# A decode step whose last weight load is cut along the partitions: six transfers over 96, 2, 4, 6, 8 and 12 partitions, the columns before it in pieces of 12 and 3

## Chip, core and metric

The kernel runs on one core of a Trainium2 chip. The metric is the device time of one execution in microseconds; before the change it is 232.49 us (median of 3 runs, 232.40 to 232.57).

## What is computed

One decode step for B = 2 tokens of width 512. The layer norm of x feeds an attention over the last 4096 cached positions (32 query heads, 8 key/value heads, head size 128) and a gated ReLU feed-forward of width 1792; both results are added to x. All data are float32. Cut to what matters:

```python
xn = _layernorm(x)
q = (xn @ wq).reshape(2, 1, 32, 128)
p = softmax(q . k_cache[last 4096] * 128 ** -0.5)
o = p . v_cache[last 4096]
h = relu(xn @ W_gate) * (xn @ W_up)
return x + o.reshape(2, 1, 4096) @ wo + h @ W_down
```

The weight wo has 4096 rows of 512 numbers, 8 MB in all.

## The kernel before

Nearly all of the 95 MB that the kernel reads (wq, the feed-forward weights, the cached keys and values, wo) are loaded by SP's DMA queue, in the order in which they are used, into a ring of four buffers (`RING = 4`, tag "ring"). A load into a buffer is issued once the work on the buffer's previous content is done. The order on TensorE is the order of the code (a manual schedule): q, gate and up, then for four groups of heads the transposes of the keys (L255), the scores (L268), the softmax and the weighted sum of the values (L332), and at the end the projections.

The end of the program is what the change touches. The tile y_ps sums everything that goes to the output: x itself (L412), 14 blocks of W_down (wd) and 32 blocks of wo. `project` (L417 to L422) adds one block with four matmuls. Each float32 matmul has two records in the trace, so a block has eight of MATMUL and eight of LDWEIGHTS: 112 each for wd, 256 each for wo. Before the last projections stand the values of the last group (`values`, L332), `gather` (L348), `finish` (L357) and `spread_heads` (L362), which makes the left-hand side oT.

wo comes in two halves, wo0 and wo1, one ring buffer each: 4 MB, 128 partitions by NJ = 16 columns of 512 numbers (a column is one block of `project`, 256 KB). wo0 comes in one transfer. wo1 comes in five, cut along the columns at 8, 12, 14 and 15 (L431 to L434):

```python
for r, cuts in ((0, (0, NJ)), (1, (0, 8, 12, 14, 15, NJ))):
    wt = ring.tile([P, NJ, D], F32, name=f"wo{r}", tag="ring")
    for j0, j1 in zip(cuts, cuts[1:]):
        nc.sync.dma_start(wt[:, j0:j1], wo_rows(r, j0, j1))
    for j in range(NJ):
        project(oT[:, r, j], wt[:, j], (r, j) == (R - 1, NJ - 1))
```

A matmul on a column waits for the transfer that brings that column, whole. After the last column VectorE copies y_ps to yo (L438) and SP stores it (L439). The transfers' completions are counted on eight semaphores that are used in turn.

Of the kernel before, what the change touches and what calls it, by code (L numbers as in the profile page):

```python
# [20 lines left out]
def kernel(  # L21
# [12 lines left out]
    nc = tc.nc  # L34
    P = 128
# [12 lines left out]
    R = HKV // C  # L48
# [20 lines left out]
    def load(name, src, shape):  # L69
        t = ring.tile(shape, F32, name=name, tag="ring")  # L70
        nc.sync.dma_start(t, src)
        return t
# [12 lines left out]
    def load_kv(cache, name, g, a):  # L85
        r, b = divmod(g, B)
        base = cache[b, r * C + 2 * a, SK - W:SK, :]
        run = J * DH
        src = bass.AP(
            tensor=cache.tensor, offset=base.offset, ap=[[run, PK], [SK * DH, 2], [1, run]]  # L90
        )
        return load(f"{name}{g}_{a}", src, [P, run])


    NJ = HQ * DH // (R * P)
# [3 lines left out]
    def wo_rows(r, j0, j1):  # L99
        rows = NJ * P  # L100
        return wo[r * rows:(r + 1) * rows, :].rearrange("(p j) e -> p j e", p=P)[:, j0:j1, :]
# [84 lines left out]
    for kc in range(KC):  # L186
        for r in range(R):
            for c in range(C):
                n = r * C + c
# [169 lines left out]
    def spread_heads(r):  # L359
        op = ps_1.tile([P, NJ, B], F32, name=f"op{r}", tag="misc")  # L360
        for e in range(NE):
            nc.tensor.matmul(  # L362
                op, spread[:, e].rearrange("h k e -> h (k e)"),
                osb[r][:, :, e * NJ:(e + 1) * NJ].rearrange("h b j -> h j b"),
                start=(e == 0), stop=(e == NE - 1),
            )
        nc.vector.tensor_copy(oT[:, r, :, :, 0], op)
# [19 lines left out]
    for a in range(NP):  # L387
        kwork(0, a, load_kv(k_cache, "k", 0, a))
    for g in range(1, NG):
        for a in range(NP):  # L390
            kt_in = load_kv(k_cache, "k", g, a)
            v_in = load_kv(v_cache, "v", g - 1, a)
            kwork(g, a, kt_in, [softmax(g - 1)] if a == 0 else [])
            if a:
                gather(g - 1, a - 1)
            elif g % B == 1 and g > 1:
                spread_heads((g - 2) // B)
            values(g - 1, a, v_in)
        gather(g - 1, NP - 1)
        finish(g - 1)  # L400
# [16 lines left out]
    def project(lhsT, w, stop):  # L417
        for e in range(Q):
            nc.tensor.matmul(  # L419
                y_ps[32 * e:32 * e + 17, :], lhsT.rearrange("p b s -> p (b s)")[:, 0:17],  # L420
                w[:, e * P:(e + 1) * P], start=False, stop=stop,
            )  # L422
# [5 lines left out]
    for k in range(FB):  # L428
        project(hT[:, k], dw[:, k], False)
    spread_heads(R - 1)  # L430
    for r, cuts in ((0, (0, NJ)), (1, (0, 8, 12, 14, 15, NJ))):  # L431
        wt = ring.tile([P, NJ, D], F32, name=f"wo{r}", tag="ring")
        for j0, j1 in zip(cuts, cuts[1:]):
            nc.sync.dma_start(wt[:, j0:j1], wo_rows(r, j0, j1))  # L434
        for j in range(NJ):
            project(oT[:, r, j], wt[:, j], (r, j) == (R - 1, NJ - 1))
    yo = work.tile([P, P], F32, name="yo", tag="yo", bufs=1)
# [30 lines left out]
```

## Time and profile before

| | |
|---|---|
| median of 3 runs | 232.49 us |
| the profiled execution's own time | 232.63 us |
| its span, first to last instruction | 230.8 us |
| TensorE busy | 180.2 us (78%) |
| VectorE, ScalarE busy | 66.3 us (29%), 48.3 us (21%) |
| data moved | 95.21 MB, 413 GB/s over the span |
| mean granted TensorE clock | 0.936 of full speed |

The span leaves out 1.8 us of the execution's time around the instructions. "PE" is TensorE's matmuls and "PEld" its weight loads, which run beside them; "SPq" is SP's sequencer, which issues the transfers. [...] "DMA share" is the mean busy share of the core's 16 DMA engines. The end of a matmul is modelled, so each record is about 0.27 us long although the next one starts earlier.

### The profile page before, as it was taken

To read this page: it belongs to the slowest core of one execution; us is meant where nothing else is said; L and a number is where in the kernel's file an instruction comes from. 1 tells how busy PE (TensorE), PEld (TensorE's weight loads), DVE (VectorE), ACT (ScalarE), POOL (GpSimd) and SP (SyncE) were. 2 spreads that over 40 slices of the span, in tenths; PEclk is the share of its full clock that TensorE was granted. 3 is DMA by queue.
4 is the path that set the end of the run, shared out by engine and by line. 5 is a ranking of instruction groups with operands and counts; after the bars stand their busy time and mean duration, and the time that the engine had idled before them with its cause. 6 is when DMAs were issued, how large, how long until landed. Compare 5 with 4: busy or idle time off the path is not lost.

```text
span 230.8 us, 4036 instructions
## 1 busy us (share of the span) xinstructions
PE 180.2 (78%) x1828; PEld 109.7 (48%) x1828; DVE 66.3 (29%) x131; ACT 48.3 (21%) x81; POOL 5.4 (2%) x21
## 2 busy tenths in 40 slices
PE   0066961749999889998899699889979964888393
PEld 0031230249666573664483566458456522247281
DVE  0320021014444561441472233158034133010000
ACT  2000100004444551440351243044033102100000
POOL 8000000000000000000000000000000000000000
PEclk9999797697999999999999799999999998899678
DMA  7999999999999999999999999999999999999980
GB/s 273 426 403 443 437 432 411 454 435 415 420 452 426 420 423 450 420 429 420 435 432 430 426 432 426 429 437 426 429 426 440 420 437 435 417 435 420 406 341 35
DMA packets 3964, 95.21 MB, mean 413 GB/s; under 512 B 452, under 2 KB 460, under 8 KB 876
## 3 DMA queue, kind: packets, MB, share of 16 engines
q1 hardware_dynamic: 3900, 94.90, 96.4%
q8 instruction: 14, 0.23, 0.4%
q10 hardware_dynamic: 48, 0.07, 0.1%
q14 instruction: 2, 0.02, 0.0%
HBM read 94.96 MB, written 0.00 MB: 412 GB/s over the span
## 4 chain that ended last, share of the span: by engine, by line
DMA 52%; PE 40%; DVE 4%; issue 1%; SPq 1%; ACT 1%
DMA k<-in_A_k_cache_dram 37%; PE pk L255 21%; DMA wo<-in_A_wo_dram 11%; PE s L268 8%; PE o L332 5%; DMA x<-in_A_x_dram 4%; PE q_ps L190 3%; PE pp L312 1%; PE oa L348 1%; SPq L434 1%; DVE kT L244 1%; DVE pt L313 1%; ACT p L301 1%; DVE on L244 0%; DVE m L277 0%
## 5 line engine op out<-in xcount | busy, mean ns | idle before, releaser
L255 PE MATMUL pk<-ident,k 128*128 128x128 f32 x512 | 68.0, 287 | 6.4 <-DMA k<-in_A_k_cache_dram 6.3
L255 PEld LDWEIGHTS pk<-ident,k 128*128 128x128 f32 x512 | 58.2, 146 | 21.2 <-issue 17.1
L244 DVE COPY kT<-pk 128x512 f32<-128x512 f32 x64 | 44.2, 691 | 52.6 <-PE pk L255 46.7
L244 ACT COPY kT<-pk 128x512 f32<-128x512 f32 x64 | 37.5, 586 | 81.5 <-PE pk L255 81.5
L332 PE MATMUL o<-v,pt 128*32 128x512 f32 x256 | 31.0, 615 | 0.0
L268 PE MATMUL s<-kT,qz 128*32 128x512 f32 x256 | 30.9, 598 | 0.0
L332 PEld LDWEIGHTS o<-v,pt 128*32 128x32 f32 x256 | 11.0, 113 | 14.6 <-issue 9.9
L190 PE MATMUL q_ps<-wq,xnT 128*32 128x512 f32 x64 | 11.9, 914 | 2.8 <-DMA wq<-in_A_wq_dram 2.3
L419 PE MATMUL y_ps<-wo,oT 128*17 128x128 f32 x256 | 10.1, 323 | 5.0 <-DMA wo<-in_A_wo_dram 4.8
L268 PEld LDWEIGHTS s<-kT,qz 128*32 128x32 f32 x256 | 7.0, 109 | 11.9 <-issue 11.5
L348 PE MATMUL oa<-on,pick 128*16 128x128 f32 x64 | 8.3, 273 | 4.1 <-DVE on L244 3.3
L419 PEld LDWEIGHTS y_ps<-wo,oT 128*17 128x17 f32 x256 | 7.9, 116 | 7.0 <-DMA wo<-in_A_wo_dram 6.0
L244 DVE COPY on<-o 128x512 f32<-128x512 f32 x4 | 2.8, 692 | 29.0 <-PE o L332 29.0
L348 PEld LDWEIGHTS oa<-on,pick 128*16 128x16 f32 x64 | 5.8, 97 | 11.1 <-DVE on L244 7.0
L177 PE MATMUL xt_ps<-ident,xn 32*128 32x32 f32 x4 | 1.0, 299 | 12.9 <-DVE xn L172 12.9
L217 PE MATMUL u_ps<-wu,xnT 128*32 128x448 f32 x32 | 4.6, 735 | 6.3 <-DMA wu<-in_B_W_up_dram 6.3
L190 PEld LDWEIGHTS q_ps<-wq,xnT 128*32 128x32 f32 x64 | 2.7, 154 | 11.3 <-issue 7.1
L244 ACT COPY on<-o 128x512 f32<-128x512 f32 x4 | 2.3, 586 | 25.5 <-PE o L332 25.5
L301 ACT ACTIVATE p<-s,nm 128x1024 f32<-128x1024 f32 x4 | 4.5, 1115 | 12.5 <-DVE nm L296 12.5
L177 PEld LDWEIGHTS xt_ps<-ident,xn 32*128 32x128 f32 x4 | 0.8, 206 | 12.8 <-issue 12.8
L312 PE MATMUL pp<-ident,p 128*128 128x128 f32 x32 | 4.9, 279 | 2.4 <-ACT p L301 1.5
L313 DVE TENSOR_TENSOR pt<-pp,own 128x512 f32<-128x512 f32 x8 | 5.4, 690 | 3.4 <-PE pp L312 3.4
(71 smaller groups left out, 61.5 us busy)
## 6 DMA issues: line engine op xcount, KB each, us to landing
k<-in_A_k_cache_dram SPq DMA_DIRECT2D x8, 4096.0 KB, 29.2
v<-in_A_v_cache_dram SPq DMA_DIRECT2D x8, 4096.0 KB, 31.2
wq<-in_A_wq_dram SPq DMA_DIRECT2D x2, 4096.0 KB, 17.5
wo<-in_A_wo_dram SPq DMA_DIRECT2D x1, 4096.0 KB, 31.5
wg<-in_B_W_gate_dram SPq DMA_DIRECT2D x1, 3584.0 KB, 30.2
wu<-in_B_W_up_dram SPq DMA_DIRECT2D x1, 3584.0 KB
wd<-in_B_W_down_dram SPq DMA_DIRECT2D x1, 3584.0 KB, 27.9
wo<-in_A_wo_dram SPq DMA_DIRECT2D x1, 2048.0 KB, 21.6
```

What stands on the lines that cost most here:

```text
L190: nc.tensor.matmul(q_ps[r][32 * c:32 * c + 32, :], xnT[:, 0, kc, :], wqt[kc // 2][:, kc % 2, n * 512:(n + 1) * 512], start=(kc == 0), stop ...
L217: nc.tensor.matmul(dst[32 * c:32 * c + 32, :], xnT[:, 1, kc, :], wt[:, kc, c * FQ:(c + 1) * FQ], start=(kc == 0), stop=(kc == KC - 1),)
L244: (nc.vector.tensor_copy if turn[0] % 2 else nc.scalar.copy)(dst, src)
L255: nc.tensor.transpose(pk[:, u * P:(u + 1) * P], kt_in[:, j * P:(j + 1) * P], ident)
L268: nc.tensor.matmul(ss[g][32 * q:32 * q + 32, :], qz[:, g, 32 * n:32 * n + 32], kt[:, h, q * 512:(q + 1) * 512], start=(a == 0 and s1 == 0 ...
L301: nc.scalar.activation(p, both, AF.Exp, bias=nm, scale=SCALE, accum_out=l)
L312: nc.tensor.transpose(pp[:, u], pv[:, lo:lo + P], ident)
L313: nc.vector.tensor_tensor(pts[g][:, jh].rearrange("p n u k -> p u n k"), pp.rearrange("p u (n k) -> p u n k", k=HK), own.rearrange("p h i ...
L332: nc.tensor.matmul(o[32 * q:32 * q + 32, :], pts[g][:, jh, n].rearrange("p u k -> p (u k)"), v[:, lo:lo + 512], start=(s1 == 0 and jh == 0 ...
L348: nc.tensor.matmul(oa[g], pick[:, u, 8 - 8 * a:24 - 8 * a], ons[a][:, u], start=(a == 0 and u == 0), stop=(a == NP - 1 and u == 3),)
L419: nc.tensor.matmul(y_ps[32 * e:32 * e + 17, :], lhsT.rearrange("p b s -> p (b s)")[:, 0:17], w[:, e * P:(e + 1) * P], start=False, stop=stop,)
L434: nc.sync.dma_start(wt[:, j0:j1], wo_rows(r, j0, j1))
```

## The change

The last column of wo1 (column 15, 256 KB) is cut along the partitions into six transfers, of 96, 2, 4, 6, 8 and 12 partitions; each brings 2 KB a partition. Columns 0 to 14 now come in two pieces, of 12 and of 3 columns, where there were four (8, 4, 2 and 1). The number of bytes, the buffers and the matmuls stay as they were.

```diff
+    LAST = (96, 2, 4, 6, 8, 12)
+    assert sum(LAST) == P
...
-    for r, cuts in ((0, (0, NJ)), (1, (0, 8, 12, 14, 15, NJ))):
+    for r, cuts in ((0, (0, NJ)), (1, (0, 12, 15, NJ))):
         wt = ring.tile([P, NJ, D], F32, name=f"wo{r}", tag="ring")
         for j0, j1 in zip(cuts, cuts[1:]):
-            nc.sync.dma_start(wt[:, j0:j1], wo_rows(r, j0, j1))
+            src = wo_rows(r, j0, j1)
+            p0 = 0
+            for n in (P,) if (r, j1) != (R - 1, NJ) else LAST:
+                nc.sync.dma_start(wt[p0:p0 + n, j0:j1], src[p0:p0 + n])
+                p0 += n
         for j in range(NJ):
             project(oT[:, r, j], wt[:, j], (r, j) == (R - 1, NJ - 1))
```

On SP, at the program's end (wo_1674 is wo0, wo_1740 is wo1; DMAHW0 to DMAHW7 are the eight semaphores of the transfers; a shape is partitions x numbers a partition):

```order
 L71 DMA wd<-in_B_W_down_dram 128x7168 [waits DMAHW1_49,PE_49]
-L434 DMA wo_1674<-in_A_wo_dram 128x8192 [waits DMAHW2_49,PE_49]
-L434 DMA wo_1740<-in_A_wo_dram 128x4096 [waits DMAHW3_49,PE_49]
-L434 DMA wo_1740<-in_A_wo_dram 128x2048
-L434 DMA wo_1740<-in_A_wo_dram 128x1024
-L434 DMA wo_1740<-in_A_wo_dram 128x512 x2
-L439 DMA out_dram<-yo 4x2x128 [waits DMAHW4_49,DVE_49]
```

```order
+L441 DMA wo_1674<-in_A_wo_dram 128x8192 [waits DMAHW2_49,PE_49]
+L441 DMA wo_1740<-in_A_wo_dram 128x6144 [waits DMAHW3_49,PE_49]
+L441 DMA wo_1740<-in_A_wo_dram 128x1536
+L441 DMA wo_1740<-in_A_wo_dram 96x512
+L441 DMA wo_1740<-in_A_wo_dram 2x512
+L441 DMA wo_1740<-in_A_wo_dram 4x512
+L441 DMA wo_1740<-in_A_wo_dram 6x512 [waits DMAHW4_49]
+L441 DMA wo_1740<-in_A_wo_dram 8x512 [waits DMAHW5_49]
+L441 DMA wo_1740<-in_A_wo_dram 12x512 [waits DMAHW6_49]
+L447 DMA out_dram<-yo 4x2x128 [waits DMAHW7_49,DVE_49]
```

The five transfers of wo1 have become eight, and three of them wait for the semaphore that they take over: the one over 6 partitions for the last load of values (DMAHW4), the one over 8 partitions for wd (DMAHW5), the one over 12 partitions for wo0 (DMAHW6).

On TensorE, the projections of wo before the change:

```order
L419 MATMUL y_ps<-wo_1674,oT 17x128 [waits DMAHW6_49]
L419 MATMUL y_ps<-wo_1674,oT 17x128 x63
L419 MATMUL y_ps<-wo_1740,oT 17x128 [waits DMAHW7_49,DVE_49]
L419 MATMUL y_ps<-wo_1740,oT 17x128 x31
L419 MATMUL y_ps<-wo_1740,oT 17x128 [waits DMAHW0_49]
L419 MATMUL y_ps<-wo_1740,oT 17x128 x15
L419 MATMUL y_ps<-wo_1740,oT 17x128 [waits DMAHW1_49]
L419 MATMUL y_ps<-wo_1740,oT 17x128 x7
L419 MATMUL y_ps<-wo_1740,oT 17x128 [waits DMAHW2_49]
L419 MATMUL y_ps<-wo_1740,oT 17x128 x3
L419 MATMUL y_ps<-wo_1740,oT 17x128 [waits DMAHW3_49]
L419 MATMUL y_ps<-wo_1740,oT 17x128 x3
```

and with it:

```order
L423 MATMUL y_ps<-wo_1674,oT 17x128 [waits DMAHW6_49]
L423 MATMUL y_ps<-wo_1674,oT 17x128 x63
L423 MATMUL y_ps<-wo_1740,oT 17x128 [waits DMAHW7_49,DVE_49]
L423 MATMUL y_ps<-wo_1740,oT 17x128 x47
L423 MATMUL y_ps<-wo_1740,oT 17x128 [waits DMAHW0_49]
L423 MATMUL y_ps<-wo_1740,oT 17x128 x11
L423 MATMUL y_ps<-wo_1740,oT 17x128 [waits DMAHW4_49,DMAHW5_49,DMAHW3_49,DMAHW6_49,DMAHW2_49,DMAHW1_49]
L423 MATMUL y_ps<-wo_1740,oT 17x128 x3
```

The matmuls are the same and stand in the same order. The waits ahead of columns 8, 12 and 14 are gone, the first wait now stands for 12 columns, and the wait ahead of column 15 is for six semaphores.

## Rows read from the trace of the kernel before

**Rows 1.** The page, 40 slices of the span: granted clock and DMA share, in tenths.

```profile
PEclk9999797697999999999999799999999998899678
DMA  7999999999999999999999999999999999999980
```

**Rows 2.** Chain of waits from 200 us: start us, us, what.

```profile
200.41 0.33 SPq L434
...
200.79 0.43 SPq L434
...
201.73 0.43 SPq L434
...
202.21 24.94 DMA wo<-in_A_wo_dram
...
227.19 0.46 PE y_ps L419 x8
```

**Rows 3.** DMA issues of wo1, in order: KB each, us from issue to landing.

```profile
wo<-in_A_wo_dram SPq DMA_DIRECT2D x1, 2048.0 KB, 21.6
wo<-in_A_wo_dram SPq DMA_DIRECT2D x1, 1024.0 KB, 23.8
wo<-in_A_wo_dram SPq DMA_DIRECT2D x1, 512.0 KB, 24.6
wo<-in_A_wo_dram SPq DMA_DIRECT2D x2, 256.0 KB, 24.9
```

**Rows 4.** Timeline of PE and SP at the end: start us, us [idle before <-releaser].

```profile
207.38 3.25 PE L419 MATMUL y_ps<-wd,hT 128*17 128x128 f32 x112
...
217.11 9.85 PE L419 MATMUL y_ps<-wo,oT 128*17 128x128 f32 x248 [4.58 <-DMA wo<-in_A_wo_dram]
...
227.19 0.41 PE L419 MATMUL y_ps<-wo,oT 128*17 128x128 f32 x8 [0.23 <-DMA wo<-in_A_wo_dram]
...
227.99 0.69 SPq L439 DMA_DIRECT2D out_dram<-yo  x1
```

**Rows 5.** Stretches: us, busy by engine (count), granted clock, DMA share, GB/s.

```profile
207.50:210.50 3.00, 3.00 (x112) 2.85 (x106) 0.34 (x1) 0.00 (x0) 0.00 (x0) 1.00 0.96 415
...
215.10:218.50 3.40, 1.39 (x28) 1.13 (x32) 0.00 (x0) 0.00 (x0) 0.00 (x0) 0.50 1.01 431
218.50:221.90 3.40, 3.40 (x72) 2.71 (x68) 0.00 (x0) 0.00 (x0) 0.00 (x0) 0.50 0.96 396
```

**Rows 6.** Stretches of the last microseconds, same columns.

```profile
222.00:223.00 1.00, 1.00 (x46) 0.99 (x40) 0.00 (x0) 0.00 (x0) 0.00 (x0) 1.00 0.99 379
223.00:224.00 1.00, 1.00 (x46) 0.99 (x40) 0.00 (x0) 0.00 (x0) 0.00 (x0) 1.00 0.73 287
224.00:225.00 1.00, 1.00 (x44) 0.96 (x40) 0.00 (x0) 0.00 (x0) 0.00 (x0) 1.00 0.47 184
225.00:226.00 1.00, 0.85 (x33) 0.57 (x28) 0.00 (x0) 0.00 (x0) 0.00 (x0) 1.00 0.38 135
```

**Rows 7.** Timeline of PE, two earlier waits for keys.

```profile
129.46 1.89 PE L255 MATMUL pk<-ident,k 128*128 128x128 f32 x9 [2.08 <-DMA k<-in_A_k_cache_dram]
...
169.55 1.50 PE L255 MATMUL pk<-ident,k 128*128 128x128 f32 x12 [1.25 <-DMA k<-in_A_k_cache_dram]
```

**Rows 8.** Stretches behind these two waits, columns as in rows 5.

```profile
130.00:133.00 3.00, 3.00 (x16) 3.00 (x15) 1.38 (x2) 0.70 (x2) 0.00 (x0) 0.50 0.94 404
133.00:134.00 1.00, 1.00 (x11) 1.00 (x10) 0.46 (x1) 0.50 (x2) 0.00 (x0) 0.92 0.99 426
...
169.60:173.00 3.40, 3.40 (x29) 3.03 (x30) 2.08 (x3) 1.59 (x3) 0.00 (x0) 1.00 0.96 414
```

**Rows 9.** Line 419's second semaphore wait: count, ns min/median/max, start us.

```profile
L419 PEldq EVENT_SEMAPHORE  x1: 51/51/51, 222.3 to 222.3; - x1
```

**Rows 10.** Waits of SP: total us, times, longest us.

```profile
SPq L463 <- DMA out_dram<-yo: 1.0, 1, 1.0
```

## Prediction

> **What bounds the kernel now.** I read the page's slices first: the 16 DMA engines are busy in tenth 9 of nearly every slice up to the last two [rows 1]. The kernel reads without a pause, and only what stands behind the reading can change the end. So the rest is read from the end: the chain of waits, the issues, the timeline of PE, and stretches of a microsecond.
>
> The chain runs through the last transfer of wo1, issued at 202.21 us and landing 24.94 us later, at 227.15; then one column's matmuls (227.19, 0.46 us), then the copy and the store [rows 2]. Those 24.94 us are queueing: the five transfers of wo1 are issued within 2 us of each other and land one after the other [rows 2, 3]. Issue times plus issue-to-landing times give the landings: columns 0 to 7 at 200.41 + 21.6 = 222.0, columns 8 to 11 at 200.79 + 23.8 = 224.6, column 14 at 201.73 + 24.8 = 226.5 (24.9 is the median of the two 256 KB pieces, and the last took 24.94), column 15 at 227.15. The pieces before the last are thus spaced so that PE has done all it can when the last 256 KB lands: at 227.19 it has one column left.
>
> [...] Less the 0.27 us of the last record, 2.98 / 111 = 26.8 ns a record, 0.215 us a column. [...] wo0's 16 columns start at 217.11, after 4.58 us of idling [rows 4], at the lower clock, which is granted until 221.9 [rows 5]: 4.79 us make 11.1 columns, the other 4.9 take 1.05 us, and with the last record's 0.25 us PE is done with wo0 at about 223.2. Before the change columns 0 to 7 have landed by then and fill the time up to the next piece.
>
> The DMA engines don't finish together. From 222 us their busy share falls, 0.99, 0.73, 0.47, 0.38 in successive microseconds [rows 6]: some have nothing left while the slowest still work on the last columns. A transfer counts as landed only with its slowest engine.
>
> **The change, part by part.**
>
> *More and smaller issues.* Eight instead of five, each about 0.43 us on SP [rows 2]. Seven of them are out by about 203.5 (200.4 + 7 x 0.45) or, if the wait for wd counts, by 208: over 15 us before their turn. The one over 12 partitions waits for wo0, whose landing lets PE start at 217.11 [rows 4], and is issued by 217.6. A small transfer that waits behind nothing is the 4 KB store: issue at 227.99, 0.69 us [rows 4], landed 1.0 us after that [rows 10], 1.7 us in all. So this one could land at 219.3 and in fact waits for its turn at 226.5. Cost 0; the cover is 7 us of queued reading.
>
> *The last column's rows.* Consecutive 256 KB pieces land 227.15 - 226.5 = 0.65 us apart, or about 0.08 us for each of the 8 rows that an even split over 16 engines gives one engine. The trace has no load over fewer than 128 partitions that shows which engines take its rows. The 96 give 6 rows to each; the five small transfers can add none to an engine or one each, so an engine has 6 to 11 rows. Between "the slowest engines lose 2" and "the slowest gain 3", the landing moves by -0.16 to +0.24 us, to between 226.99 and 227.39. I take 0 for the sum, since the next term is later than either. [...]
>
> *The columns before it.* This is the term that counts. The first wait on wo1 is now for 12 columns. They are the same bytes as the two first pieces before and land when the second one did, at 224.6. From 223.2 to 224.6 PE now has nothing to do, and it then owes 12 columns where it owed 4. From 224.63 (landing to first matmul takes 0.04 us, 227.15 to 227.19) the 16 columns of wo1 run as one train, if their data keep up: 128 records, 3.25 + 16 x 0.0268 = 3.68 us, to 228.31. They do keep up: column 12 is reached at 224.63 + 12 x 0.215 = 227.21, and its piece lands at 226.5; column 15 is reached at 227.86, and lands by 227.39 at the latest. PE's last matmul ended at 227.19 + 0.41 = 227.60 [rows 4]; now it ends at 228.31, **0.71 us later**. Copy and store follow as before.
>
> Bounds: if the train starts 0.1 us earlier (issue times and rounded landings don't tell less), +0.6; at 3.25 / 14 = 0.232 us a column the train takes 3.71, +0.74.
>
> *Six semaphores at column 15.* An instruction that waits for two has one extra wait, of 51 ns, on PE's weight-load queue at 222.3 [rows 9], about 0.6 us ahead of wo1's first matmul (wo0's columns ran until about 223), without a gap in the timeline. Five extra take 0.25 us; run ahead in the same way they cost 0, otherwise 0.25. I take 0.
>
> **Sum**: +0.71, with bounds +0.6 and +1.0. The profiled execution goes from 232.63 to 233.34; it lies 0.14 above the median of the runs, so the median goes from 232.49 to 233.20. A measurement of this kernel tells about 0.2%, 0.46 us, from no change, so that should show as slower.
>
> **The rivals.**
>
> *The clock falls (slower still).* The new idle time is about 1.4 us, and afterwards PE has 3.7 us of work with nothing to hide it. After 1.25 us of idling at 168.3 the clock stayed at 1.00; after 2.08 us at 127.4 it went to 0.50 for 130 to 133 and back within the next microsecond [rows 7, 8]. Ours is nearer to the 1.25. But an execution in which the low stretch ahead of 221.9 ends earlier would have wo0 done by 217.11 + 16 x 0.215 + 0.25 = 220.8 and idle 3.8 us, near the 4.58 us that were followed by 0.50 [rows 4, 5]. A low stretch of 3.4 us (as 218.5 to 221.9) does half its work and costs 1.7 us more: 233.2 + 1.7 = 234.9. Chance 0.10.
>
> *The transfer still ends last (not slower).* If PE isn't late, the time follows the landing, -0.16 to +0.24: 232.3 to 232.7. For this, PE must have done 15 columns when the last lands: the 12 columns must be there by 227.15 - 0.16 - 15 x 0.215 - 0.04 = 223.7, or the matmuls must run 0.7 us faster in all. For it speaks that most engines have finished before 225 [rows 6], so that little holds the 12 columns back; against it, that this little is the slowest engine, for which nothing of the first 12 columns changes. Chance 0.13, nearly all of it within 0.2%. That the small transfers don't shift rows between engines as they are meant to belongs here too: it alone changes nothing, since column 15 has 227.86 - 227.15 = 0.7 us to spare.
>
> *Small transfers in sequence (slower).* If each of the five paid its own 1.0 us [rows 10], one after the other, behind the one over 96 partitions, column 15 would land near 226.5 + 0.5 + 5 x 1.0 = 232.0 and the time be about 237.3. It decides once the landing passes 227.86. Against it: two 256 KB pieces in the queue land 0.65 us apart, about what their bytes take. Chance 0.03. [...]
>
> **How the numbers follow.** The forecast has 0.74 with +0.6 to +1.0 (233.1 to 233.5), all of it beyond 0.2%. With the clock's 0.10 and the sequence's 0.03, slower has 0.87. The transfer's 0.13 gives 0.11 to no change, and 0.02 to faster, for a tail that gains more than two rows. The range 232.4 to 234.0 holds the forecast and nearly all of the transfer's case, some 0.85; the fallen clock lies above it.
>
> **What would show it.** Right: PE idle about 1.4 us before the first matmul on wo1 at 224.6; then one train of 128 records without a gap, in 3.7 us; yo's copy released by PE with column 15's data there before; a chain that ends in about 3.7 us of PE behind the transfer of 12 columns, no longer in the last transfer. Wrong: a wait for wo ahead of the last eight records, as now; a granted clock of 0.50 after 224.6; a last landing after 227.9; the first matmul on wo1 well ahead of 224.6.

## The result and the profile after

The changed kernel takes 233.40 us (median of 4 runs, 233.33 to 233.86) where the kernel before took 232.44 in the same comparison: a ratio of 1.0045, 95% interval 1.0028 to 1.0062, so 0.96 us or 0.4% slower. The profiled execution took 233.46 us with a span of 231.6.

The end of the changed kernel's chain of waits (start us, us, what), which answers to [rows 2]:

```profile
201.86 22.95 DMA wo<-in_A_wo_dram
224.81 0.14 issue
224.94 3.72 PE y_ps L423 x128
```

The chain leaves the transfers with the landing of the 12 columns (issued at 201.86, landed at 224.81) and ends in one train of 128 records on TensorE. Before, it stayed with the transfers to 227.15 and had eight records behind them.

PE's timeline there, with the idle time in front, against [rows 4]:

```profile
216.84 5.72 PE L423 MATMUL y_ps<-wo,oT 128*17 128x128 f32 x128 [2.97 <-DMA wo<-in_A_wo_dram]
...
224.94 3.69 PE L423 MATMUL y_ps<-wo,oT 128*17 128x128 f32 x128 [2.39 <-DMA wo<-in_A_wo_dram]
```

wo0's columns are done at 222.56, then TensorE stands still for 2.39 us, then works 3.69 us without a gap to 228.63; before it ended at 227.60. TensorE does not stand still ahead of column 12 or of column 15.

Stretches of the changed kernel, columns as in [rows 5]:

```profile
215.10:221.00 5.90, 4.16 (x80) 3.34 (x84) 0.00 (x0) 0.00 (x0) 0.00 (x0) 0.50 0.98 420
221.20:224.80 3.60, 1.36 (x52) 1.07 (x40) 0.00 (x0) 0.00 (x0) 0.00 (x0) 1.00 0.78 266
224.90:228.60 3.70, 3.65 (x128) 3.44 (x128) 0.00 (x0) 0.00 (x0) 0.00 (x0) 1.00 0.18 59
```

The granted clock stayed at 1.00 through the idle time and the train behind it. And one row that the prediction did not look for:

```profile
223.00:224.00 1.00, 0.00 (x0) 0.00 (x0) 0.00 (x0) 0.00 (x0) 0.00 (x0) 1.00 0.43 102
```

At a busy share of 0.43 the DMA engines moved 102 GB/s. Divided by the share, that is 237 GB/s for 16 busy engines (below: "for a full share"); before, in the same microsecond, 0.73 moved 287, that is 393 [rows 6]. Busy engines moved 0.6 of what they did.

The trace's packets say which pieces were slow; a packet here is one partition's row of a piece. Up to 222 us each packet of the 12 columns (24 KB, all 128 partitions) took 0.92 us. The last five, which start from 222.67 on, took 1.33 to 1.57 us, while other engines were already at column 15. So engines that are still on pieces over 128 partitions are slowed as well.

### The profile page after: what moved, and what is told of

Read it like the earlier page. It is cut to its first block, busy times and chain, and to the rows that moved or that the text cites. A ratio compares the mean times of both kernels' runs of the same rounds, so it can differ in the third digit from the quotient of the medians.

```text
span 231.6 us, 4042 instructions
## 1 busy us (share of the span) xinstructions
PE 182.8 (79%) x1828; PEld 110.2 (48%) x1828; DVE 66.4 (29%) x131; ACT 48.3 (21%) x81; POOL 5.4 (2%) x21
## 4 chain that ended last, share of the span: by engine, by line
PE 53%; DMA 38%; DVE 5%; ACT 2%; issue 1%
DMA k<-in_A_k_cache_dram 24%; PE pk L259 23%; PE s L272 11%; DMA wo<-in_A_wo_dram 10%; PE o L336 9%; DMA x<-in_A_x_dram 4%; PE q_ps L194 3%; PE pp L316 2%; PE y_ps L423 2%; ACT p L305 2%; PE oa L352 2%; DVE kT L248 1%; PE op L366 1%; DVE on L248 1%; DVE pt L317 1%
## 5 line engine op out<-in xcount | busy, mean ns | idle before, releaser
L272 PE MATMUL s<-kT,qz 128*32 128x512 f32 x256 | 32.1, 618 | 0.0
L336 PE MATMUL o<-v,pt 128*32 128x512 f32 x256 | 32.1, 634 | 0.0
L194 PE MATMUL q_ps<-wq,xnT 128*32 128x512 f32 x64 | 11.4, 880 | 3.2 <-DMA wq<-in_A_wq_dram 2.7
L423 PE MATMUL y_ps<-wo,oT 128*17 128x128 f32 x256 | 9.4, 317 | 5.4 <-DMA wo<-in_A_wo_dram 5.4
L352 PEld LDWEIGHTS oa<-on,pick 128*16 128x16 f32 x64 | 5.8, 97 | 11.1 <-DVE on L248 7.0
L221 PE MATMUL u_ps<-wu,xnT 128*32 128x448 f32 x32 | 5.9, 918 | 6.3 <-DMA wu<-in_B_W_up_dram 6.3
```

What stands on the lines that cost most here:

```text
L194: nc.tensor.matmul(q_ps[r][32 * c:32 * c + 32, :], xnT[:, 0, kc, :], wqt[kc // 2][:, kc % 2, n * 512:(n + 1) * 512], start=(kc == 0), stop ...
L221: nc.tensor.matmul(dst[32 * c:32 * c + 32, :], xnT[:, 1, kc, :], wt[:, kc, c * FQ:(c + 1) * FQ], start=(kc == 0), stop=(kc == KC - 1),)
L272: nc.tensor.matmul(ss[g][32 * q:32 * q + 32, :], qz[:, g, 32 * n:32 * n + 32], kt[:, h, q * 512:(q + 1) * 512], start=(a == 0 and s1 == 0 ...
L336: nc.tensor.matmul(o[32 * q:32 * q + 32, :], pts[g][:, jh, n].rearrange("p u k -> p (u k)"), v[:, lo:lo + 512], start=(s1 == 0 and jh == 0 ...
L352: nc.tensor.matmul(oa[g], pick[:, u, 8 - 8 * a:24 - 8 * a], ons[a][:, u], start=(a == 0 and u == 0), stop=(a == NP - 1 and u == 3),)
L423: nc.tensor.matmul(y_ps[32 * e:32 * e + 17, :], lhsT.rearrange("p b s -> p (b s)")[:, 0:17], w[:, e * P:(e + 1) * P], start=False, stop=stop,)
```

## Experiments

Each ratio is to the kernel before in the same group of runs (medians 232.33 to 232.39 us). Each profile is of one execution.

**The two halves of the change apart.** First the six transfers with the old cuts:

```diff
-    for r, cuts in ((0, (0, NJ)), (1, (0, 12, 15, NJ))):
+    for r, cuts in ((0, (0, NJ)), (1, (0, 8, 12, 14, 15, NJ))):
```

> The old cuts at 8, 12, 14 and 15 with the new six transfers for column 15: the split along the partitions alone. Theory (the added time is TensorE's, which gets its first columns of wo1 only at 224.6): TensorE again has one column left when the last transfer lands, so the time follows the landing and moves by -0.16 to +0.35 us against before: 232.3 to 232.8, a wait for wo ahead of the last eight records. Rival (the six small transfers cost the time, one after the other or through their later landing): about 233.4, as with the whole change.

Measured: 233.05 us, 1.0031 (1.0020 to 1.0042). A miss: the split alone costs 0.66 us. The end of its chain, and its microsecond 223 to 224:

```profile
225.04 2.65 DMA wo<-in_A_wo_dram
...
227.73 0.46 PE y_ps L423 x8
```

```profile
223.00:224.00 1.00, 0.94 (x37) 0.75 (x29) 0.00 (x0) 0.00 (x0) 0.00 (x0) 1.00 0.78 186
```

The transfer is last again, as expected, but its column is started at 227.73 instead of 227.19, 0.54 us later. The DMA engines are slow here too (238 GB/s for a full share). In this kernel wo1 has nine transfers, and the ninth, over 12 partitions, is issued only at 225.04, once columns 8 to 11 have landed. The completions in the trace tell this second effect from the first: the transfer over 96 partitions landed at 227.55, the ninth at 227.69, so that at most 0.14 of the 0.54 us is the second effect's. Column 14, which is whole, landed at 227.16 instead of 226.5. The runs with two or four transfers in place of six don't have the second effect.

Then the new cuts with column 15 whole:

```diff
-            for n in (P,) if (r, j1) != (R - 1, NJ) else LAST:
+            for n in (P,):
```

> The new cuts at 12 and 15 with column 15 in one transfer: the coarser pieces alone. Theory: the same train of 128 records behind the landing of 12 columns, about 233.4 (233.2 to 233.6), no wait ahead of column 15. Rival (the small transfers cost the time): 232.4 to 232.6.

Measured: 233.14 us, 1.0030 (1.0019 to 1.0041). As the theory said, with the same train and no slow stretch:

```profile
224.28 3.72 PE y_ps L423 x128
```

```profile
223.00:224.00 1.00, 0.00 (x0) 0.00 (x0) 0.00 (x0) 0.00 (x0) 0.00 (x0) 1.00 0.51 205
```

At a share of 0.51 the engines move 205 GB/s, 402 for a full share. The last five packets of the 12 columns took 0.92 us here, but for one of 1.41. So each half costs about 0.7 us alone, and both together 0.96, not 1.4: in the whole change the later landing of column 15 lies under the train. In these two executions the train begins 0.66 us later with the split (224.94 for 224.28), and the slower packets account for about 0.4 of it (an estimate: 1.33 for 0.92). That the split adds time to the whole change is not clear of the noise, since the intervals overlap (1.0028 to 1.0062 with it, 1.0019 to 1.0041 without).

**One cut given back.** Cuts at 8, 12 and 15 with the six transfers:

```diff
-    for r, cuts in ((0, (0, NJ)), (1, (0, 12, 15, NJ))):
+    for r, cuts in ((0, (0, NJ)), (1, (0, 8, 12, 15, NJ))):
```

> The changed kernel with one cut more, at column 8 (8, 4, 3 and 1 columns, the last in six transfers). Theory: 8 columns land at about 222 and are done before the next 4 land at 224.6 to 224.8; these take 0.9 us, the next 3 land at about 226.6 and take 0.7, to 227.3; then only column 15 is left, landed by 227.5 at the latest: 232.4 to 232.8, the added time gone to within 0.3 us. Rival (the six transfers cost it): about 233.4.

Measured: 233.21 us, 1.0034 (1.0023 to 1.0045), a miss for the same reason. Its profiled execution took 444.53 us, the other eight 232.88 to 233.85, so its page shows nothing of this program's usual end. The same kernel was run again:

> Cuts at 8, 12 and 15 with the six transfers once more, for a profile that can be read. The time was 0.82 us above before where 0 to 0.3 was expected. Theory: TensorE is no longer the last (it waits for column 15), and what is left is the split's later landing, 0.4 us or more behind the 227.15 of before; about 233.0 to 233.2. Rival: TensorE still works without a gap from the landing of columns 8 to 11 on, and ends last.

Measured: 233.02 us, 1.0033 (1.0021 to 1.0045), as the theory said. PE's timeline at its end (this execution took 233.74 us, the longest of its five):

```profile
227.33 0.85 PE L423 MATMUL y_ps<-wo,oT 128*17 128x128 f32 x24 [1.14 <-DMA wo<-in_A_wo_dram]
228.40 0.41 PE L423 MATMUL y_ps<-wo,oT 128*17 128x128 f32 x8 [0.22 <-DMA wo<-in_A_wo_dram]
```

TensorE waits for columns 12 to 14 and again for 15: with one more cut the train is gone. The time is that of the split alone (233.05 us).

**A shorter train without touching the transfers.**

```diff
-            project(oT[:, r, j], wt[:, j], (r, j) == (R - 1, NJ - 1))
+            if (r, j) not in [(1, i) for i in range(8)]:
+                project(oT[:, r, j], wt[:, j], (r, j) == (R - 1, NJ - 1))
```

> The changed kernel without the matmuls of columns 0 to 7 of wo1 (8 of wo's 32 blocks are left out of the sum; all transfers stay as they are). TensorE then owes 4 columns, not 12, when the first piece lands. Theory (the length of TensorE's train sets the end): 4 columns are done by 225.8, the next 3 by about 227.3, and the landing of column 15 ends last again: 232.4 to 232.8. Rival A (the late landing of the coarse piece or of the small transfers costs the time, whatever TensorE has to do): about 233.4. Rival B (a clock that falls in the longer idle time): above 233.

Measured: 233.56 us, 1.0050 (1.0031 to 1.0068): the least clear of the runs. PE's timeline and the stretch at the end of its profiled execution:

```profile
225.12 1.07 PE L423 MATMUL y_ps<-wo,oT 128*17 128x128 f32 x32 [2.69 <-DMA wo<-in_A_wo_dram]
...
227.22 1.73 PE L423 MATMUL y_ps<-wo,oT 128*17 128x128 f32 x32 [1.03 <-DMA wo<-in_A_wo_dram]
```

```profile
227.20:229.00 1.80, 1.73 (x32) 1.18 (x32) 0.00 (x1) 0.00 (x0) 0.00 (x0) 0.57 0.03 9
```

The train is cut in two by a wait for columns 12 to 14, as the theory has it. But with 2.69 and 1.03 us of idling and 1.07 of work between them the granted clock fell, and the last 32 records took 1.73 us, where the 32 before them took 1.07. This is rival B, in a kernel that idles more than the change does. It is not all: at the full clock the last 32 records would have ended at 227.22 + 1.07 = 228.29, still 0.69 us later than before, because columns 12 to 14 landed at about 227.2 and not at 226.5. So rival A has a share too. That the train sets the end is shown by the new cuts with column 15 whole, against the kernel before; this run does not show it.

**Why the split is slow.** Two transfers of 96 and 32 rows, both multiples of 16 (old cuts, as in all that follow). That each engine then has 6 and 2 of them is an estimate from an even split:

```diff
-    LAST = (96, 2, 4, 6, 8, 12)
+    LAST = (96, 32)
```

> The old cuts, column 15 in two transfers, over 96 and over 32 partitions; both counts are multiples of 16, so each engine again has 6 + 2 = 8 rows. The question is why the split alone cost 0.66 us. In its profile the microsecond 223 to 224 has a DMA share of 0.78 at 186 GB/s, where before had 0.73 at 287: engines are busy and move less. Theory A (two engines that write the same group of partitions slow each other, and a transfer over 96 or fewer partitions hands the rows to other engines than one over 128): the even counts don't help, the same slow stretch appears, 232.8 to 233.2. Theory B (small transfers on few engines, or the uneven counts, cost it): no slow stretch, 232.3 to 232.5.

Measured: 233.00 us, 1.0029 (1.0018 to 1.0041). The slow stretch is there:

```profile
223.00:224.00 1.00, 1.00 (x48) 0.98 (x40) 0.00 (x0) 0.00 (x0) 0.00 (x0) 1.00 0.61 168
```

275 GB/s for a full share, with counts that divide by 16 and no transfer under 32 partitions: theory B falls. The slow stretch needs no small transfers.

The same six sizes, with the small ones at the lowest partitions:

```diff
-            p0 = 0
+            p0 = P - LAST[0] if (r, j1) == (R - 1, NJ) else 0
...
-                p0 += n
+                p0 = (p0 + n) % P
```

> The old cuts and the same six transfers in the same order and sizes, but the one over 96 takes partitions 32 to 127 and the five small ones take 0 to 31. Theory A (engines that write the same partitions slow each other; the slowest engines are among the upper ones and fill the upper partitions in all other pieces): the early engines' small rows no longer go where the slow engines write, so part of the loss goes: 232.5 to 232.9, and a slow stretch that is shorter than with the small ones on top. Theory B (number and size of the small transfers, whichever partitions): as with the small ones on top, about 233.05.

Measured: 232.97 us, 1.0022 (1.0012 to 1.0032), between the two expectations and hardly better than with the small ones on top:

```profile
223.00:224.00 1.00, 1.00 (x40) 0.95 (x36) 0.00 (x0) 0.00 (x0) 0.00 (x0) 0.94 0.76 203
```

267 GB/s for a full share. Moving the rows down did not free the slow engines, which speaks against theory A in the form that it had.

Two halves along the row instead of along the partitions:

```diff
-            for n in (P,) if (r, j1) != (R - 1, NJ) else LAST:
-                nc.sync.dma_start(wt[p0:p0 + n, j0:j1], src[p0:p0 + n])
+            for lo, hi in ((0, D),) if (r, j1) != (R - 1, NJ) else ((0, D // 2), (D // 2, D)):
+                nc.sync.dma_start(wt[:, j0:j1, lo:hi], src[:, :, lo:hi])
```

> The old cuts, column 15 in two transfers along the numbers of a row (256 and 256) over all 128 partitions: more and smaller transfers with every row on the engine it had. Theory A: no slow stretch, landing as before, and only half of the last column's matmuls behind it: 232.3 to 232.5. Theory B (a smaller last transfer costs time by itself): 232.7 or more.

Measured: 232.26 us, 0.9994 (0.9985 to 1.0003), no difference from before, and no slow stretch:

```profile
223.00:224.00 1.00, 1.00 (x45) 0.98 (x38) 0.00 (x0) 0.00 (x0) 0.00 (x0) 1.00 0.65 247
```

380 GB/s for a full share. Halving the transfer along the row cost nothing here (0.9994); taking fewer than 128 partitions did (1.0029 for 96 and 32). That every row stayed on the engine it had is the author's assumption; no row shows it.

Four transfers of 32 partitions, then the same with all four sent to partitions 0 to 31, then the same as the first but read from other rows:

```diff
-    LAST = (96, 2, 4, 6, 8, 12)
+    LAST = (32, 32, 32, 32)
```

> The old cuts, column 15 in four transfers over 32 partitions each (0 to 31, 32 to 63, 64 to 95, 96 to 127); two rows of each for every engine, 8 in all, as in one transfer. The pair to the next run. Theory A (rows that reach a group of partitions from another engine than the one that fills it otherwise slow that one): a stretch at 223 to 224 with few GB/s at a high DMA share, as with 96 and 32; 232.8 to 233.3. Theory B (the counts of rows or few engines cost it): 232.3 to 232.5.

Measured: 233.25 us, 1.0036 (1.0025 to 1.0046), 184 GB/s at a share of 0.65 (283 for a full share).

```diff
+    low = ktp.tile([32, 4, D], F32, name="low", tag="kT")
...
+                dst = wt[p0:p0 + n, j0:j1] if n == P else low[:, p0 // 32:p0 // 32 + 1]
+                nc.sync.dma_start(dst, src[p0:p0 + n])
...
```

> The same four transfers, from the same rows of wo and in the same order, but all four write partitions 0 to 31 of another tile, side by side; the last four matmuls read a quarter of each (column 15 is thus not added rightly: three quarters of its rows are left out of every output). Only the destination differs from the run before. Theory A with the destination as the cause: the engines that finish first, the lower ones, are slowed by the writes to their own partitions, where they have 3 us to spare; the slow ones are not: columns 8 to 14 land as in before and so does column 15, 232.2 to 232.6. Theory C (the source is the cause, reads of neighbouring rows of wo by other engines): as the run before, 232.8 to 233.3.

Measured: 233.58 us, 1.0041 (1.0028 to 1.0053).

```profile
223.00:224.00 1.00, 0.47 (x17) 0.29 (x6) 0.00 (x0) 0.00 (x0) 0.00 (x0) 1.00 0.72 168
```

```profile
227.13 1.03 PE L423 MATMUL y_ps<-wo,oT 128*17 128x128 f32 x24 [1.42 <-DMA wo<-in_A_wo_dram]
228.09 0.87 PE L450 MATMUL y_ps<-low,oT 32*17 32x128 f32 x8
```

233 GB/s for a full share. The time can't be set beside the other runs', since the four new matmuls (L450) take 0.87 us where column 15 takes 0.41. The landings can: columns 12 and 13, which go to all 128 partitions as ever, are waited for until 227.13; before, even column 14 had landed at 226.5. Theory A expected those columns on time, and falls as it stands. It took for granted that the slowest engines fill the upper partitions, which no row here shows.

```diff
+            if (r, j1) == (R - 1, NJ):
+                src = w_down[0:P, :].rearrange("(p j) e -> p j e", j=1)
```

> The four transfers over 32 partitions with their own destinations, as two runs before, but read from 128 rows of W_down that lie one behind the other (256 KB in one piece) instead of from rows of wo that lie 32 KB apart (column 15 of wo is thus replaced by other numbers in every output). Only the source differs. The run with another destination was as slow, so the destination alone is not the cause. Theory C (the source: neighbouring rows, 32 KB apart, read at one time by different engines, hold up each other and the other reads): no stretch with few GB/s, 232.2 to 232.6. Theory D (a transfer over fewer than 128 partitions is slow beside others whatever it reads or writes): the same slow stretch at 223 to 224, 232.9 to 233.4.

Measured: 233.19 us, 1.0037 (1.0023 to 1.0051).

```profile
223.00:224.00 1.00, 1.00 (x48) 0.99 (x40) 0.00 (x0) 0.00 (x0) 0.00 (x0) 1.00 0.67 180
```

269 GB/s for a full share from a source in one piece: theory C falls too. What the slow kernels share is that a transfer takes a range of fewer than 128 partitions. The last run measures that by itself, in large loads away from the end:

```diff
+    PARTS = {"wu": (32, 32, 32, 32), "wd": (64, 64), "wo0": (96, 32)}
...
+        for n in PARTS.get(name, (P,)):
+            nc.sync.dma_start(dst[p0:p0 + n], src[p0:p0 + n])
+            p0 += n
...
```

> Neither the destination nor the source took the slow stretch away. This one asks whether a transfer over fewer partitions is slow by itself, away from the end: the kernel before with three of its big loads cut along the partitions, W_up (3.67 MB) in 32 + 32 + 32 + 32, W_down in 64 + 64, wo0 (4.19 MB) in 96 + 32; wo1 as before. Before, these stretches run at 415 to 445 GB/s. Theory D1 (a range of 32 or 64 partitions takes in only about half of what 128 do, as the 168 to 203 GB/s of the slow stretches suggest): some 215 GB/s while W_up and W_down are loaded, about 8.5 us more for each, and up to 5 us for wo0; 250 to 256 us. Theory D2 (only the mixture at the end, where engines that are ahead work on cut pieces beside engines that are still on whole ones): no stretch below 390 GB/s and 232.4 to 233.5 us.

Measured: 265.42 us, 1.1423 (1.1389 to 1.1456): D1, and beyond its range. The rate in 40 slices of its span, and three stretches (W_up in 32s; W_down in 64s; the first of the two transfers of wo0, over 96):

```profile
GB/s 319 408 408 433 383 192 218 353 401 426 448 401 458 413 432 438 406 448 416 448 427 418 448 411 428 443 421 443 411 438 433 246 212 208 208 214 177 237 363 34
```

```profile
32.20:36.20 4.00, 3.90 (x28) 1.35 (x32) 0.00 (x0) 0.00 (x0) 0.00 (x0) 0.59 1.10 222
```

```profile
221.00:229.00 8.00, 0.00 (x0) 0.00 (x0) 0.00 (x0) 0.00 (x0) 0.00 (x0) 0.50 1.02 207
230.00:244.00 14.00, 6.34 (x116) 5.70 (x108) 0.21 (x1) 0.00 (x0) 0.00 (x0) 0.62 0.98 195
```

All 16 engines are busy, at about 210 GB/s where 128 partitions run at 415 to 445. Halved rates for 3.67, 3.67 and 4.19 MB make about 27 of the 33 us (11.5 MB at 210 instead of 425 GB/s); where the other 6 come from was not followed up. The expectation for wo0 was too low: 96 partitions (195 GB/s) are as slow as 64 (207). That the rate halves is shown; the reason is not, neither for 32 and 64 partitions nor for 96.

## Why the prediction was right, point by point

**The train.** The step that counted held. Forecast: 128 records from 224.63 to 228.31, in 3.68 us. Profile: 224.94 to 228.63, in 3.69. The new cuts alone, without the split, made the same train (1.0030). The forecast's 26.8 ns a record and 0.215 us a column are worked out from wd's 112 records in 3.25 us at a granted clock of 1.00 [rows 4, 5], less 0.27 us for the last of them. For its 11.1 columns in 4.79 us a column takes 0.43 us at a clock of 0.50, twice that. Two stretches of wo's records before the change show the factor, 84 in 4.00 us at 0.50 and 84 in 2.00 us at 1.00 (us, PE, PEld, granted clock, DMA share, GB/s):

```profile
217.60:221.60 4.00, 4.00 (x84) 3.18 (x80) 0.50 0.97 405
222.10:224.10 2.00, 2.00 (x84) 1.98 (x76) 1.00 0.84 325
```

**Its start.** 0.31 us later than forecast, so TensorE's last matmul ended 1.03 us later than before, not 0.71. (The medians are 0.96 apart and the two profiled executions 0.83; single executions don't tell these apart.) Two statements failed. The first stands under the second rival: "the slowest engine, for which nothing of the first 12 columns changes". It does change: the twelve columns landed at 224.81, not 224.6, and their last packets took 1.33 to 1.57 us instead of 0.92, as other engines had come to the cut pieces. How much of the landing is due to that stays open, since the same bytes landed at 224.6 before and at 224.15 with the new cuts alone.

The second is that an extra semaphore wait costs nothing. The first matmul came 0.14 us behind the landing, not 0.04. The 0.04 was read at column 15, where one semaphore is waited for; the first wait on wo1 is for two. Before, its extra wait ran ahead at 222.3, while wo0's columns were still being worked on [rows 9]; here TensorE was idle, and it stands behind the landing:

```profile
L423 PEldq EVENT_SEMAPHORE  x4: 51/51/51, 224.8 to 227.8; - x4
```

**The idle time ahead of it.** Forecast about 1.4 us, measured 2.39. wo0's columns began 0.27 us earlier and had the full clock from about 221, not 221.9, so that they were done at 222.56 instead of 223.2, and the landing was later. The length of the train doesn't depend on this.

**The last column's rows.** Forecast at -0.16 to +0.24 us for the landing, from row counts alone. The trace has 2, 4, 6, 8 and 12 completions for the small transfers, where one over 128 partitions has 16; as far as that tells, each ran on as many engines as it has partitions. Before, the 16 completions of column 15 came from 223.63 to 227.15 us, each 0.64 to 0.66 us behind one of column 14 (both in order of time), which fits 8 rows for each engine; the first matmul on it started at 227.19, behind the last of them. That the 96 rows give each engine 6 is an estimate from an even split. What the row counts left out is the rate. With the old cuts, where nothing covers it, column 15 starts 0.54 us later (227.73 for 227.19), out of the bounds, and 96 and 32 rows, which divide by 16, cost as much in the time (1.0029 for 1.0031). In the changed kernel, by the completions in its trace, columns 12 to 14 landed at 227.11 (forecast: 226.5) and column 15 at 227.50 (forecast: 227.39 at the latest). The train reached them at about 227.52 and 228.17, so the sum did not suffer; for columns 12 to 14, with 0.4 us to spare, that was luck. The rate of a transfer over fewer partitions was a cost that the trace of before could not show.

**The rivals.** *The clock falls*: not in the change, whose clock stayed at 1.00 after 2.39 us of idling; it fell where eight columns of work were taken out (0.57 over the last 1.80 us). The argument against it was that 1.4 us is nearer to 1.25 than to 2.08. At 2.39 us the argument speaks for a fall, and that the clock held was luck. The rival's price, 1.7 us, took a low stretch of 3.4 us; rows 5 show 0.50 over both stretches before 221.9, 6.8 us, so it was priced too low. *The transfer still ends last*: not in the change; with the cut at 8 given back it does, but late. *Small transfers in sequence*: the five do not pay one after the other (column 15 was there at 227.50, not at 232.0), and 96 and 32 cost as much as the six (1.0029 for 1.0031); what parts cost is the rate, about half in large loads (195 to 222 GB/s for 415 to 445).

**Issues and semaphores.** The eight issues stayed hidden. The six semaphores ahead of column 15 left no gap in the train: of the four records above, three belong to them, and they ran ahead by 227.8.

## What to carry to other kernels

Where the last load is cut into pieces so that work follows it closely, count the work that is still owed at each landing: a piece whose work takes longer than what is left to transfer (here 12 columns at 0.22 us behind a landing 2.5 us before the end, and four more columns after them) ends last, however early the last bytes are there. Cut such loads along the row, over all 128 partitions: two halves along the row cost nothing here (0.9994), while parts of 32, 64 or 96 partitions ran at about half the rate (195 to 222 GB/s for 415 to 445), and pieces over 128 partitions that moved beside such parts were slowed (1.33 to 1.57 us a packet for 0.92). Evening out the engines' finishing times by giving some fewer partitions therefore lost more here (0.66 us with the old cuts) than the two rows of 0.08 us that the slowest engines could have been spared.

## What was not expected

Transfers over 32, 64 or 96 partitions ran at 195 to 222 GB/s with all engines busy, against 415 to 445 for 128. The clock kept 1.00 after 2.39 us of idling in one execution, where 2.08 us had been followed by 0.50 in another [rows 7, 8]; the length of one idle time does not tell it. No version here beats the kernel before beyond its noise; a split of rows between engines that keeps every transfer on 128 partitions was not tried.
